# Four attention layers of 32 query heads: attention begins with a quarter of the keys, output products go in passes, and TensorE's order comes from other assumed durations

## The chip, the cores and the metric

The kernel runs on one core of a Trainium2 chip. The metric is the device time of one execution in microseconds (us). The kernel before takes 4103.47 us, the median of three runs (4100.76 to 4105.26). One further execution was profiled; its own time is 4101.9 us.

## The reference

The input x has 2048 rows of 512 numbers. Four layers follow one another; they use the weights A, B, A, B. A layer is x + attention(layernorm(x)) @ wo, with 32 query heads of 16 numbers each, and one head of keys and one of values that all query heads share:

```python
q = (x @ wq).reshape(B, S, H, Dh).transpose(0, 2, 1, 3)    # 32 heads of 16
k = x @ wk                                                  # one head of 16
v = x @ wv
p = softmax(einsum("bhqd,bkd->bhqk", q, k) * Dh ** -0.5)
o = einsum("bhqk,bkd->bhqd", p, v)                          # 2048 x 2048 per head
```

Per layer there are 32 x 2048 x 2048 exponentials, 134 million, and they are computed without a running maximum; a check at the end chooses a general path for inputs whose scores are too large, and that path does not run here.

## The kernel before, in words

A layer's queries are cut into four blocks of 512 rows (b = 0 to 3) and the 32 heads into four groups of eight (m = 0 to 3); a block and a group make a *pair*, and there are 64 pairs. The 2048 keys are cut into sixteen *key chunks* of 128. In a pair, even and odd heads are taken in turn (`odd`), four heads each; a pair and a parity with a range of key chunks is a *segment* (`segs`). For one key chunk of one segment there are:

- two *score steps* (S, in `scores`, line 500): each multiplies 128 keys with the queries of two heads, two matmuls side by side, into a tile `st` of 128 x 1024 in PSUM, of which there are three (NST);
- two exponentials on ScalarE (line 505), one for each `st`, 4096 in the whole kernel, into a tile `pt`, of which there are seven (NPT);
- one *value step* (P, in `pv`, line 520): eight matmuls that read the two `pt` and add four heads' products, with the sum of the exponentials beside them, to one bank `acc` of PSUM.

When a segment ends, `merge` adds `acc` to `num` and `den` on VectorE; after the pair's last segment it takes the reciprocal and writes `ot`.

Everything else is *background*: generators whose steps are put between S and P. A step of type M is three matmuls (`mm3`, lines 213 to 215), since float32 operands are split in two parts. `outputs` multiplies `ot` with wo (one M for each group and 128 rows), adds to the tile `xt` (line 364) and writes x to DRAM; `normed` does the layer norm of a block and four transposing steps (T, line 257); `keys_values` makes a block's keys and values in four M, one norm step (N, line 207) and one transposing step (V, line 304), with a chain on VectorE between; `queries` makes four M and an N for each group, writes them to DRAM, and `load_q` (line 383, eight DMAs on SyncE's queue) brings them back in the layout that S reads. `load_x` loads a block's x into four of six `xt` tiles, also on SyncE's queue.

The order of TensorE's instructions is written out when the program is built, by a loop that keeps a clock of its own: it adds an assumed duration for each step (`T_MM`, `T_S`, `T_P`), assumes when exponentials end (`T_EXP`), and chooses S, P or a background step. A background step may go ahead when `credit` is positive (each P earns RATE), while the first block of a layer still lacks its values (`urgent`), or when both S and P would have to wait (`stall`). `Background` has two queues, `first` and `later`; `need(key)` runs steps, `first` ahead of `later`, until the key is there, whatever the credit. Engines run their instructions in program order, so an instruction that waits holds up those behind it.

Before the loop, a preamble computes the normed rows of blocks 0 to 2, their keys and values, and the queries of pair 0. In each layer, the pair (b = 0, m = 0) is cut at key chunk 12, so that the last block's keys may come later.

Of the kernel before, what the change touches and what calls it, by code (L numbers as in the profile page):

```python
# [20 lines left out]
P = 128  # L21
S = 2048
# [12 lines left out]
NPT = 7  # L35
# [11 lines left out]
T_MM, T_S, T_P, T_EXP, SYNC, LATE = 225, 216, 1090, 973, 180, 270  # L47
RATE = 300


class Clock:


    def __init__(self):
        self.pe = 0
        self.dve = 0

    def mm(self, ns):
        self.pe += ns
# [5 lines left out]
class Background:  # L65
# [3 lines left out]
    def __init__(self, clk):  # L69
# [6 lines left out]
        self.ready = 0  # L76

# [3 lines left out]
    def add_later(self, *gens):  # L81
        self.later.extend(gens)

# [3 lines left out]
    def step(self):  # L87
        while self.left():
            if not self.open:
                self.queue = self.first or self.later  # L90
            try:
                self.clk.pe = max(self.clk.pe, self.ready)
                self.open, self.ready = next(self.queue[0])
# [18 lines left out]
def fast_path(ctx, tc, x_in, weights, out, flag):  # L112
# [7 lines left out]
    pts = ctx.enter_context(tc.tile_pool(name="pts", bufs=NPT))  # L120
# [77 lines left out]
    def copy(dst, src):  # L198
        if state["pool"] is None:
            V.tensor_copy(dst, src)  # L200
        else:
            nc.scalar.copy(dst, src)  # L202
# [8 lines left out]
    def mm3(ps, a, b, first, last):  # L211
# [4 lines left out]
        clk.mm(3 * T_MM)  # L216
# [3 lines left out]
    ot = {}  # L220

# [46 lines left out]
    def keys_values(l, b):  # L268

        i = l % 2  # L270
        xT = xnT[l, b]

# [5 lines left out]
        kf = one.tile([P, BQ], F32, name="kf")  # L278
# [36 lines left out]
    def queries(l, b, ms=range(NM), last=True):  # L315
# [5 lines left out]
        yield False, clk.dve + SYNC  # L321
        for m in ms:
# [25 lines left out]
            yield False, at  # L348

    def outputs(l, b, ms):  # L350

        w = wt["wo", l]
        yield False, clk.dve + SYNC
        last = NM - 1 in ms
        for t in range(4 * b, 4 * b + 4):
# [17 lines left out]
            if last and t == 4 * b + 3:  # L373
                bg.done.add(("x", l, b))
            yield False, clk.dve + SYNC
# [50 lines left out]
    slots = [(s, c, j) for s, (_, _, c0, c1) in enumerate(segs) for c in range(c0, c1)  # L426
             for j in (0, 2, 1, 3)]
    qt = {}
# [4 lines left out]
    def merge(s):  # L433
# [6 lines left out]
        if pr not in sums:  # L440
            sums[pr] = [one.tile([P, BQ], F32, name=n) for n in ("num", "den")]
# [10 lines left out]
        r = one.tile([P, BQ], F32, name="rec")  # L452
        if (l, b) > (0, 0):
            bg.need(("x",) + ((l, b - 1) if b else (l - 1, NB - 1)))
# [12 lines left out]
        if m == NM - 2:  # L467
            load_x(l, b)
        if b < NB - 1:
            if m == NM - 1:  # L470
                bg.add(outputs(l, b, range(NM)))
                if l < NL - 1:
                    bg.add(normed(l + 1, b), keys_values(l + 1, b))
                    bg.add_later(queries(l + 1, b))
        elif m == NM - 2:
            bg.add(outputs(l, b, range(NM - 1)))
        elif m == NM - 1:
# [280 lines left out]
```

## Time and profile before

| What | Value |
|---|---|
| median of 3 runs | 4103.47 us |
| the profiled execution's own time | 4101.9 us |
| its span on the core | 4100.1 us |
| TensorE (PE) matmul busy | 3916.7 us, 96% |
| ScalarE (ACT) busy | 3815.2 us, 93% |
| VectorE (DVE) busy | 1115.5 us, 27% |
| GpSimd (POOL) busy | 90.9 us, 2% |
| first exponential starts, last one starts | 60.5 us, 4079.4 us |

Busy time counts the stretch in which at least one instruction of the engine is under way. Matmuls overlap, and the end of one is modelled, so a TensorE that is 96% busy need not be working at its peak; distances from start to start say more. An exponential, too, may start while the one before it is still under way: its mean duration is 1314 ns, but 4096 of them make 3805.3 us of busy time.

### The profile page before, as it was taken

What the parts mean: (1) busy time and instruction counts of PE and PEld (TensorE: products, weight loads), DVE (VectorE), ACT (ScalarE), POOL (GpSimd) and SP (SyncE); (2) the same over time, 40 slices, a digit from 0 to 9 for tenths busy, and PEclk for the clock granted to TensorE, in tenths of its full rate; (3) what the DMA queues carried; (4) which work ended last, traced back from release to release, by engine and by line L of the source; (5) the groups of instructions that cost most, each with busy time, mean ns of one, the idle gap of its engine ahead of it and who ended that gap; (6) DMA issues with size and microseconds to landing.
All of it is one profiled execution on the core that took longest, in us unless ns stands there. A gap on an engine that the chain in (4) does not pass through costs nothing.

```text
span 4100.1 us, 65070 instructions
## 1 busy us (share of the span) xinstructions
PE 3916.7 (96%) x26707; PEld 1043.3 (25%) x26707; DVE 1115.5 (27%) x1770; ACT 3815.2 (93%) x4112; POOL 90.9 (2%) x101
## 2 busy tenths in 40 slices
PE   6999999999999999999999999999999999999998
PEld 3232222222221222222222222222222222121212
DVE  6333313232331321313233122131324211011112
ACT  4999999999999999999999999999999999999997
POOL 1000000000000000000000000000000000000000
PEclk8999999999999999999999999999999999999999
DMA  2010100000001000000001000000000100000000
GB/s 79 19 39 27 37 16 16 27 21 27 27 19 34 21 32 14 14 27 22 32 22 47 6 22 32 21 16 19 22 29 24 34 11 32 6 21 22 16 21 12
DMA packets 85877, 100.92 MB, mean 25 GB/s; under 512 B 14144, under 2 KB 63296, under 8 KB 85568
## 3 DMA queue, kind: packets, MB, share of 16 engines
q1 hardware_dynamic: 85248, 95.60, 7.1%
q8 instruction: 212, 3.47, 0.3%
q0 software_dynamic: 320, 1.05, 0.1%
q14 instruction: 97, 0.79, 0.1%
HBM read 63.05 MB, written 33.55 MB: 24 GB/s over the span
## 4 chain that ended last, share of the span: by engine, by line
PE 54%; ACT 35%; issue 8%; DVE 3%; DMA 0%; ACTq 0%; POOL 0%; SPq 0%; DVEq 0%; POOLq 0%
ACT pt L505 35%; PE acc L520 23%; PE st L500 17%; PE qps L213 2%; PE ops L213 2%; PE qps L214 1%; PE qps L215 1%; PE ops L214 1%; PE ops L215 1%; PE tps L257 1%; PE gps L207 1%; PE kps L213 0%; PE kps L214 0%; PE kps L215 0%; DVE ko L291 0%
## 5 line engine op out<-in xcount | busy, mean ns | idle before, releaser
L505 ACT ACTIVATE pt<-st 128x1024 f32<-128x1024 f32 x4096 | 3805.3, 1314 | 219.9 <-PE st L500 205.6
L520 PE MATMUL acc<-pt,vop 128*32 128x512 f32 x16384 | 2167.6, 604 | 4.5 <-DVE gv L309 4.5
L500 PE MATMUL st<-qt,kop 64*128 64x512 f16 x8192 | 1491.5, 383 | 131.7 <-ACT pt L505 3.3
L500 PEld LDWEIGHTS <-kop 64*128 64x128 f16 x8192 | 368.4, 93 | 2201.8 <-issue 2183.2
L520 PEld LDWEIGHTS acc<-pt,vop 128*32 128x32 f32 x16384 | 331.5, 108 | 587.8 <-issue 579.2
L446 DVE SCALAR_TENSOR_TENSOR num<-acc,half,num 128x512 f32<-128x512 f32 x72 | 54.1, 751 | 1048.5 <-PE acc L520 1048.5
L461 DVE RECIPROCAL den<-den 128x512 f32<-128x512 f32 (+1 forms) x76 | 216.3, 2847 | 2.2
L364 DVE TENSOR_TENSOR xt<-ops,xt 128x512 f32<-128x512 f32 x76 | 52.5, 691 | 565.4 <-PE ops L215 565.4
L443 DVE TENSOR_SCALAR num<-acc,half 128x512 f32<-128x512 f32 x64 | 48.0, 751 | 540.7 <-PE acc L520 540.7
L330 DVE TENSOR_SCALAR q<-qps 128x512 f32<-128x512 f32 x64 | 44.2, 691 | 492.5 <-PE qps L215 492.5
L213 PE MATMUL qps<-xnT,wq 128*128 128x512 f32 x256 | 119.1, 465 | 0.8 <-ACT xnT L202 0.7
L213 PE MATMUL ops<-wo,ot 128*128 128x512 f32 x252 | 116.7, 463 | 2.0 <-DVE xt L364 2.0
L214 PE MATMUL qps<-xnT,wq 128*128 128x512 f32 x256 | 101.9, 398 | 0.2 <-DVE xnT L262 0.2
L215 PE MATMUL qps<-xnT,wq 128*128 128x512 f32 x256 | 101.4, 396 | 0.0
L214 PE MATMUL ops<-wo,ot 128*128 128x512 f32 x252 | 99.4, 394 | 0.0
L215 PE MATMUL ops<-wo,ot 128*128 128x512 f32 x252 | 98.7, 392 | 0.0
L332 POOL TENSOR_TENSOR sq<-q 128x512 bf16<-128x512 f32 x64 | 66.5, 1039 | 1442.4 <-DVE q L330 1442.4
L337 DVE SCALAR_TENSOR_TENSOR q<-gps,q 128x512 f32<-128x512 f32 x64 | 44.1, 689 | 110.1 <-PE gps L207 110.1
L257 PE MATMUL tps<-ident,xn 128*128 128x128 f32 x256 | 44.3, 304 | 26.6 <-DVE xn L247 26.6
L213 PEld LDWEIGHTS qps<-xnT,wq 128*128 128x128 f32 x256 | 48.3, 189 | 65.1 <-issue 46.1
L213 PEld LDWEIGHTS ops<-wo,ot 128*128 128x128 f32 x252 | 47.0, 187 | 57.0 <-issue 46.0
L200 DVE CAST xnT<-tps 128x512 fp32r<-128x512 f32 x52 | 35.9, 690 | 71.1 <-PE tps L257 71.1
(91 smaller groups left out, 1108.8 us busy)
## 6 DMA issues: line engine op xcount, KB each, us to landing
qt<-qs SPq DMA_DIRECT2D x512, 64.0 KB, 2.3
qs<-qs SPq DMA_DIRECT2D x64, 256.0 KB, 2.1
xs<-xt SPq DMA_DIRECT2D x48, 256.0 KB, 2.0
xt<-xs SPq DMA_DIRECT2D x48, 256.0 KB, 3.9
xt<-in_A_x_dram SPq DMA_DIRECT2D x32, 256.0 KB, 3.6
out_dram<-xt SPq DMA_DIRECT2D x16, 256.0 KB, 2.1
wst<-in_A_wo_dram SPq DMA_DIRECT2D x8, 256.0 KB, 2.7
wst<-in_B_wq_dram SPq DMA_DIRECT2D x8, 256.0 KB, 3.0
```

The source lines that it names most:

```text
L213: PE.matmul(ps, a[0], b[0], start=first, stop=False)
L214: PE.matmul(ps, a[0], b[1], start=False, stop=False)
L215: PE.matmul(ps, a[1], b[0], start=False, stop=last)
L257: PE.transpose(ps[:, c * P:(c + 1) * P], xn[:, c * P:(c + 1) * P], ident)
L332: G.tensor_tensor(sq, q, q, ALU.mult)
L364: V.tensor_tensor(x, ps, x, ALU.add)
L443: V.tensor_scalar(t, a, k, None, ALU.mult)
L446: V.scalar_tensor_tensor(t, a, k, t, ALU.mult, ALU.add)
L461: V.reciprocal(den[:, c], den[:, c])
L500: PE.matmul(st[:, k * 512:(k + 1) * 512], kop[l % 2][c // 4][r, (c % 4) * P:(c % 4 + 1) * P], qt[pr][r, 2 * (j % 2) + odd], start=True, st ...
L505: nc.scalar.activation(pt[:, :n], st[:, :n], AF.Exp, scale=SCALE / UP / UP)
L520: PE.matmul(acc[s][32 * j:32 * j + 32, :], vop[l % 2][c // 4][:, c % 4, 16 * odd:16 * odd + 32], pt[:, k * 512:(k + 1) * 512], start=(c == ...
```

## The change

- The planner's durations: S (`T_MM`) 216 ns, an M's matmul (`T_MR`) 231, P 860 (was 1090), the distance of exponentials 904 (was 973), and a table CHANGE of what a change between S, P and M adds. A step is chosen only if, by the planner's clock, TensorE is back at S before ScalarE runs out (`fits`, with 100 ns of slip). The old rules (`stall`, `fed`, `last_p`) go.
- `segs`: in layer 0 the three pairs of block 0 with m = 0 to 2 take turns over four quarters of the keys; in layers 1 to 3 the pairs m = 0 and 1 of block 0 take turns, key chunks 0 to 11 and then 12 to 15. `num` and `den` have three buffers for it, and a pair's queries are loaded again for each turn.
- The preamble makes only block 0's normed rows, keys and values, and pair 0's queries; blocks 1 to 3 go to the background.
- `outputs` goes in passes: groups 0 and 1 after m = 1, groups 2 and 3 after m = 3 (in block 3, group 2 and group 3 by themselves). `load_x` goes from the merge of m = 2 to that of m = 1. `hurry` moves the next block's `queries` from `later` to the end of `first`, ahead of the `normed` that is added then.
- `pt` is one tile with eight slots, and the dependency of an exponential on the one eight before it is dropped.

```diff
-NPT = 7
+NPT = 8
-T_MM, T_S, T_P, T_EXP, SYNC, LATE = 225, 216, 1090, 973, 180, 270
-RATE = 300
+T_MM, T_MR, T_P, T_EXP, T_END, LEAD, SYNC, LATE = 216, 231, 860, 904, 1020, 487, 60, 270
+CHANGE = {"SP": 93, "PS": 114, "SM": 200, "PM": 200, "MS": 105, "MP": 105}
+RATE, SLIP = 300, 100
...
+    def mm(self, ns, mode="M"):
+        self.pe += self.change(mode) + ns
+        self.mode = mode
+
+    def act(self):
+        self.exp.append(max(self.exp[-1] + T_EXP if self.exp else 0, self.pe - T_MM + LEAD))
...
+    def hurry(self, gen):
+
+        if gen in self.later:
+            self.later.remove(gen)
+            self.first.append(gen)
...
-    for pr, (l, b, m) in enumerate(pairs):
-        cuts = [0, NK]
-        if b == 0 and m == 0:
-            cuts = [0, 12, NK]
-        for c0, c1 in zip(cuts, cuts[1:]):
-            for odd in range(2):
-                segs.append((pr, odd, c0, c1))
+    for l in range(NL):
+        first = 16 * l
+        n, cuts = (3, [0, 4, 8, 12, NK]) if l == 0 else (2, [0, 12, NK])
+        segs += [(p, odd, c0, c1) for c0, c1 in zip(cuts, cuts[1:]) for p in range(first, first + n)
+                 for odd in range(2)]
+        segs += [(p, odd, 0, NK) for p in range(first + n, first + 16) for odd in range(2)]
...
-        if m == NM - 2:
+        last = b == NB - 1
+        if m == 1:
             load_x(l, b)
...
+            bg.add(outputs(l, b, [0, 1]))
+        elif m == 2 and last:
+            bg.add(outputs(l, b, [2]))
+        elif m == 3:
+            bg.add(outputs(l, b, [3] if last else [2, 3]))
             if l < NL - 1:
+
+                bg.hurry(qs_of[l + (b + 1) // NB, (b + 1) % NB])
+                bg.add(normed(l + 1, b), keys_values(l + 1, b))
...
-            if j == 0 and c == (0 if pr else 12) and odd and pr + 1 < len(pairs):
-                qt.pop(pr - 1, None)
-                qt[pr + 1] = load_q(*pairs[pr + 1])
+            if j == 0 and s in loads and c == c1 - 3:
+                qt[segs[s + 1][0]] = load_q(*pairs[segs[s + 1][0]])
...
+        if len(exps) >= NPT:
+            tc.declare_no_dep(e, exps[-NPT], reason="behind the reads in between")
...
-        for b in range(NB - 1):
-            run(kv[b], NC)
-            if b == 0:
-                run(q0)
-            if b < NB - 2:
-                run(normed(0, b + 1))
-            run(kv[b])
+        run(kv[0], 1 + NC)
+        run(q0)
+        run(kv[0])
...
-        bg.add(queries(0, 0, range(1, NM)), normed(0, 3), kv[3],
-               load_split(("wo", 0), weights[0][3]))
+        bg.add(queries(0, 0, [1, 2], False))
+        for b in range(1, NB):
+            if b == NB - 1:
+                bg.add(queries(0, 0, [3]))
+            bg.add(normed(0, b), kv[b])
+        bg.add(load_split(("wo", 0), weights[0][3]))
...
+            urgent = b == 0 and ("v", l, NB - 1) not in bg.done
+            now = clk.pe
+
+            free = sum(e + T_END + SYNC <= now for e in clk.exp[nxt - NST:]) if nxt >= NST else NST
+            s_at = max(now, clk.exp[nxt - NST] + T_END + SYNC) if nxt >= NST else now
+            dry = clk.exp[-1] + T_EXP - LEAD if clk.exp else now
...
+            def fits(mode, ns):
+                return now + clk.change(mode) + ns + CHANGE[mode + "S"] <= max(dry, s_at) + SLIP
+
+            near = c > c1 - 1 - (bg.size + 2) // 2
+            m_ok = bg.can() and (not near or bg.open) and (
+                urgent or credit > 0 or min(s_at, p_at) > now + 300 or near and bg.open)
+            if forced:
+                what = "P"
+            elif free and (clk.mode == "S" or free > 1):
+                what = "S"
+            elif m_ok and fits("M", 3 * T_MR):
+                what = "M"
+            elif p_at <= now and fits("P", T_P):
+                what = "P"
+            elif free:
+                what = "S"
```

More of the change, by code (lines that the diff above doesn't have):

```diff
@@ L92, in step @@
                 self.clk.pe = max(self.clk.pe, self.ready)
-                self.open, self.ready = next(self.queue[0])
+                self.open, self.ready, *size = next(self.queue[0])
+                if not self.open:
+                    self.size = size[0] if size else 1
                 return True
@@ L220, in fast_path @@
     ot = {}
+    qs_of = {}
     def load_x(l, b):
@@ L277, in keys_values @@
                 yield True, clk.pe
-        kf = one.tile([P, BQ], F32, name="kf")
+        kf = one.tile([P, BQ], F32, name="tmp")
         V.stream_shuffle(kf, ps, upper)
@@ L372, in outputs @@
                     xt[l + 1, t] = x
-            if last and t == 4 * b + 3:
-                bg.done.add(("x", l, b))
-            yield False, clk.dve + SYNC
+            if t == 4 * b + 3:
+                bg.done.update(("o", l, b, m) for m in ms)
+            yield False, clk.dve + SYNC, len(ms)
     def load_q(l, b, m):
@@ L440, in merge @@
         if pr not in sums:
-            sums[pr] = [one.tile([P, BQ], F32, name=n) for n in ("num", "den")]
+            sums[pr] = [one.tile([P, BQ], F32, name=f"{n}{pr % 3}") for n in ("num", "den")]
             for t, k in zip(sums[pr], f):
@@ L570, in fast_path @@
             l, b, m = pairs[pr]
-            urgent = b == 0 and m == 0 and ("v", l, NB - 1) not in bg.done
-            s_at = max(clk.pe, exp_end[nxt - NST] + SYNC if nxt >= NST else 0)
-            p_at = max(clk.pe, exp_end[chunk_of[ready[0]]] + SYNC) if ready else 1e12
-            forced = ready and chunk_of[ready[0]] <= nxt - NPT
-            stall = min(s_at, p_at) > clk.pe + 100
-            fed = exp_end[-1] - clk.pe if exp_end else 0
-            due = credit > 0 and (not last_p or credit > 2000) or urgent or stall
@@ L578, in fast_path @@
-            if bg.can() and (c < c1 - 3 and due or bg.open and (c >= c1 - 3 or due)):
-                before = clk.pe
-                bg.step()
-                credit -= clk.pe - before
-                last_p = False
-            elif (nxt == len(chunks) or forced or (s_at > clk.pe + 60 and p_at < s_at)
-                  or last_p and p_at <= clk.pe and fed >= T_P + W // 2 * T_S + LATE):
-                last_p = True
+            urgent = b == 0 and ("v", l, NB - 1) not in bg.done
+            now = clk.pe
@@ new lines, in fast_path @@
+            free = sum(e + T_END + SYNC <= now for e in clk.exp[nxt - NST:]) if nxt >= NST else NST
+            s_at = max(now, clk.exp[nxt - NST] + T_END + SYNC) if nxt >= NST else now
+            dry = clk.exp[-1] + T_EXP - LEAD if clk.exp else now
+            if nxt == len(chunks):
+                free, s_at, dry = 0, 1e12, 1e12
+            p_at = max(now, clk.exp[chunk_of[ready[0]]] + T_END + SYNC) if ready else 1e12
+            forced = ready and chunk_of[ready[0]] <= nxt - NPT + 1
+            def fits(mode, ns):
+                return now + clk.change(mode) + ns + CHANGE[mode + "S"] <= max(dry, s_at) + SLIP
@@ new lines, in fast_path @@
+            near = c > c1 - 1 - (bg.size + 2) // 2
[11 more added lines that the diff above has]
+                what = "S"
+            elif p_at < s_at:
+                what = "P" if fits("P", p_at - now + T_P) or s_at > 1e11 else "S"
+            else:
+                what = "S"
@@ L586, in fast_path @@
+            if what == "M":
+                bg.step()
+                credit -= clk.pe - now
+            elif what == "P":
                 clk.pe = p_at
```

67 lines of the change are left out of this document (32 added, 35 removed).

## The prediction

> **What bounds the kernel now.** I first read the whole span, then ScalarE, because the 4096 exponentials are the longest work that can't be shortened here.
>
> ```profile
> PE 3916.7 (96%) x26707; PEld 1043.3 (25%) x26707; DVE 1115.5 (27%) x1770; ACT 3815.2 (93%) x4112; POOL 90.9 (2%) x101
> L505 ACT ACTIVATE pt<-st x4096: 1017/1150/1807, 60.5 to 4079.4; 128x1024 f32<-128x1024 f32 x196
> ```
> ```profile
> 2507.45 100.94 ACT L505 ACTIVATE pt<-st 128x1024 f32<-128x1024 f32 x110 [2.60 <-PE st L500]
> 3233.18 123.85 ACT L505 ACTIVATE pt<-st 128x1024 f32<-128x1024 f32 x135 [1.90 <-PE st L500]
> ```
>
> The first exponential takes 1.02 us and ends at 61.5. In the two unbroken rows each further one adds (123.85 - 1.02) / 134 = 0.9166 us, in the other row the same. So the floor of ScalarE is 4095 x 0.9167 = 3753.9 us. The last exponential ends at about 4080.6, so from first end to last end it takes 4019.1 us: **265 us are lost there**, 61.5 us pass before, 19.5 after it, and 1.8 us lie outside the span (4101.9 against 4100.1). The planner's new 904 ns is a little less than this 917.
>
> Where the 265 us are lost, I read from windows cut at the layers (the second fence counts only M steps, by their first matmul):
>
> ```profile
> 61.00:1091.00 1030.00, 999.01 (x6803) 281.33 (x6801) 301.40 (x459) 953.78 (x1025) 32.09 (x31) 1.00 0.08 26
> 1091.00:2098.00 1007.00, 976.32 (x6686) 257.00 (x6685) 280.20 (x434) 953.58 (x1026) 20.65 (x20) 1.00 0.07 24
> 2098.00:3104.00 1006.00, 975.34 (x6680) 256.79 (x6676) 280.17 (x434) 952.56 (x1026) 20.65 (x20) 1.00 0.07 24
> 3104.00:4080.00 976.00, 928.63 (x6419) 224.49 (x6412) 192.47 (x275) 944.18 (x1024) 5.16 (x5) 1.00 0.06 20
> 2230.00:2340.00 110.00, 102.94 (x723) 21.69 (x721) 23.18 (x31) 110.00 (x122) 0.00 (x0) 1.00 0.11 32
> ```
> ```profile
> 61.00:1091.00 1030.00, 83.28 (x184) 34.60 (x183) 1.00 0.08 26
> 1091.00:2098.00 1007.00, 67.20 (x144) 26.85 (x144) 1.00 0.07 24
> 3104.00:4080.00 976.00, 38.79 (x84) 15.67 (x84) 1.00 0.06 20
> ```
>
> A layer has 1024 exponentials, 938.7 us at the floor. The layers take 1030, 1007, 1006 and 976: losses of 91, 68, 67 and 37. In the window at 2230, which has no background, ScalarE is busy for all of 110.00 us: nothing is lost. The loss comes with the background. The ScalarE row at 2507 shows how: 2.60 us of idle time, ended by a score. What TensorE did before it:
>
> ```profile
> 2500.61 0.39 PE L207 MATMUL gps<-sq,bones 128*128 128x512 bf16 x1
> 2500.94 0.39 PE L500 MATMUL st<-qt,kop 64*128 64x512 f16 x2
> 2501.26 1.06 PE L520 MATMUL acc<-pt,vop 128*32 128x512 f32 x8
> 2502.25 0.61 PE L500 MATMUL st<-qt,kop 64*128 64x512 f16 x4
> 2502.79 0.50 PE L213 MATMUL qps<-xnT,wq 128*128 128x512 f32 x1
> ...
> 2503.70 1.06 PE L520 MATMUL acc<-pt,vop 128*32 128x512 f32 x8
> 2504.69 0.50 PE L213 MATMUL qps<-xnT,wq 128*128 128x512 f32 x1
> ...
> 2506.96 0.82 PE L500 MATMUL st<-qt,kop 64*128 64x512 f16 x6
> ```
> ```profile
> 2405.20 0.65 PE L257 MATMUL tps<-ident,xn 128*128 128x128 f32 x4
> 2405.78 0.39 PE L500 MATMUL st<-qt,kop 64*128 64x512 f16 x2
> ```
>
> P and three M in a row, from 2503.70 to 2506.96, with no score between. From starts to starts: a P costs 0.99 us, two S with the change to what follows 0.54, an M between S and P 0.91, three M in a row 2.27 (0.76 each), N 0.33, T 0.58. S to a change takes 0.32 (2500.94 to 2501.26), so S to S is 0.54 - 0.32 = 0.22.
>
> **TensorE's need.** Per P there are two S and two exponentials: 0.99 + 0.54 = 1.53 us, against 1.833 on ScalarE. So TensorE has 0.30 us left per P, 155 us for a layer's 512. A lone M between two S adds 0.32 + 0.91 - 0.22 = 1.01, between S and P 0.91; I take 0.99, since the new order mostly puts it behind a first S, and 0.76 as its other end. The background of layers 1 and 2 is 144 M x 0.99 = 142.6 us; 20 N and 4 V (bounded by N) at 0.32 + 0.33 - 0.22 = 0.43, and 16 T at 0.68, make 21. Sum 164 against 155: TensorE is short by 9 us per layer if each M stands alone, and by nothing if a third stand in rows. Layer 3 has 84 M, 83 us: no shortage. Layer 0 has 184, and 8 more come from the preamble (blocks 1 and 2's keys): 190, with some 40 N and V and 24 T 223, short by 68. But 48 M that are the next layer's queries can move on, from layer to layer, into layer 3's slack. What stays short is 68 + 9 + 9 - 48 = **about 38 us**, where 265 are lost now. That is the room for another order.
>
> **The change, part by part.**
>
> *Earlier start.* The path to the first score:
>
> ```profile
> 18.23 0.50 PE L213 MATMUL qps<-xnT,wq 128*128 128x512 f32 x1 [0.68 <-ACT xnT L202]
> 23.58 0.66 DVE L189 SCALAR_TENSOR_TENSOR wq<-wst,wq 128x512 fp32r<-128x512 f32 x1
> 24.84 0.69 DVE L330 TENSOR_SCALAR q<-qps 128x512 f32<-128x512 f32 x1
> 26.07 0.86 DVE L247 TENSOR_SCALAR xn<-xt,mv,rstd 128x512 f32<-128x512 f32 x1
> 27.18 0.68 DVE L337 SCALAR_TENSOR_TENSOR q<-gps,q 128x512 f32<-128x512 f32 x1
> 31.02 0.68 DVE L262 TENSOR_TENSOR xnT<-tps,xnT 128x512 fp32r<-128x512 f32 x1
> 32.33 0.38 SPq L346 DMA_DIRECT2D qs<-qs  x1
> 34.46 3.61 SPq L383 DMA_DIRECT2D qt<-qs  x8
> 37.30 0.68 DVE L296 SCALAR_TENSOR_TENSOR kop<-gps,ko 128x512 f16<-128x512 f32 x1
> 59.70 0.68 PE L500 MATMUL st<-qt,kop 64*128 64x512 f16 x2 [2.32 <-DVE gv L309]
> ```
> ```profile
> qt<-qs SPq DMA_DIRECT2D x512, 64.0 KB, 2.3
> ```
>
> Pair 0's queries are in place at 34.46 + 3.61 + 2.3 = 40.4, block 0's keys at 38.0; the 19 us until 59.70 are blocks 1 and 2. Between 24.84 and 32.33 VectorE also works for them, 0.86 + 0.68 in the rows at 26.07 and 31.02. Without that I put the first score at 38.7, and the first exponential's end, 1.8 later as now, at 40.5: **21 us less**. Bounds: 18 (VectorE saves nothing) to 24.
>
> What is moved costs elsewhere. Its M, N, T are in the need above. Its chain is now in the loop, as block 3's is today:
>
> ```profile
> 87.75 1.40 SPq L225 DMA_DIRECT2D xt<-in_A_x_dram  x3
> 97.20 0.65 PE L257 MATMUL tps<-ident,xn 128*128 128x128 f32 x4 [2.65 <-DVE xn L247]
> 115.97 0.69 DVE L296 SCALAR_TENSOR_TENSOR kop<-gps,ko 128x512 f16<-128x512 f32 x1
> ```
>
> From the loads of x at 87.75 to the keys at 116.7 it takes 29 us. The first quarter gives ScalarE 48 exponentials, 44 us, and before this chain the queue holds two groups of queries, some 8 us each by the rows 24.84 to 32.33: 45 us. And a group of four M may begin only at the first P of a segment of four key chunks (`near`), which adds waits. So the second quarter begins late; I take 8 us. Pair 1's queries have 16 exponentials, 14.7 us, and need 4 M (2.8), 7.5 on VectorE and GpSimd, 2.1 to write, 5.9 to load: 18, late by 3. The load of x, for which TensorE's T waited 2.65 us in the row at 97.20, comes three times instead of once; it stands ahead of pair loads on SyncE's queue: 7. With about 3 of slow clock (below) the start costs **21 us** (10 to 40).
>
> *The planner's order.* It puts an M only where S can follow before ScalarE runs dry. Its prices: S S P 1499 (the rows: 1530), exponentials 904 (917), M alone 998 (990). The first two are low by 1 to 2%, so they nearly cancel. RATE lets it place 300 ns of background per P, just what TensorE has left. But one block of layers 1 and 2 needs, at its own prices, 36 x 998 + 5 N x 737 + 4 T x 951 + V, 44 us, and gets 128 x 300 = 38. The 6 us left over, queries for the most part since they stand in `later`, are forced at the block's end by `load_q`'s `need`, in a row: 6 M, then N behind GpSimd's and VectorE's 2 us. All S and P stand behind that N on TensorE, and ScalarE holds at most three scores. I take 3 us at each of 12 block ends: **36** (0, if `min(s_at, p_at) > now + 300` gives enough free places, to 100). The rows bunched there are cheap: about 80 M at 0.76 instead of 0.99 return some 20 of the 38, which leaves **18** of shortage (0 to 38).
>
> *Layer ends.* The last block's chain (merge, outputs, norm, keys) has 48 P, 88 us, before key chunk 12 is wanted; it had 24, 44 us. Its length was 29 us from a load of x, and here some 10 us of merge and outputs stand ahead: hidden by S and P of two pairs. Uncovered, it would cost up to 40. I keep **5** for three ends.
>
> *At nothing.*
>
> ```profile
> L364 DVE TENSOR_TENSOR xt<-ops,xt 128x512 f32<-128x512 f32 x76 | 52.5, 691 | 565.4 <-PE ops L215 565.4
> L446 DVE SCALAR_TENSOR_TENSOR num<-acc,half,num 128x512 f32<-128x512 f32 x72 | 54.1, 751 | 1048.5 <-PE acc L520 1048.5
> ```
>
> The passes of `outputs` add 64 additions on line 364 and the shorter segments 22 merges of two operations each, 44 + 33 us of VectorE, hidden by its 73% idle time; the M are as many as before. Fifteen more loads of queries (3.61 us of SyncE each) stand beside an idle queue. Seven to eight `pt`, and the dropped dependency: ScalarE waited for itself 4.3 us in all, so 0 to 5, taken as 0:
>
> ```profile
> ACT pt L505 <- ACT pt L505: 4.3, 19, 0.3
> ```
>
> One tile with eight slots could make every exponential wait for every P; but in this trace the first query M starts before the last piece of wq is written, so slices are followed one by one.
>
> *The tail* (19.5) is the same work.
>
> **Sum.** 40.5 + 3753.9 + (21 + 36 + 18 + 5 = 80) + 19.5 + 1.8 = **3896 us**. The profiled execution is 1.6 us below the median of the runs; I correct nothing for it.
>
> **A rule against a row.** After the idle time ahead of 59.70 the clock was low:
>
> ```profile
> 60.00:70.00 10.00, 9.31 (x43) 4.81 (x41) 1.93 (x4) 5.08 (x6) 1.04 (x1) 0.74 0.00 0
> ```
>
> At 0.74 of ten us, with the rest full, 2.6 us of work were lost, my 3 above. The Trainium skill ("TensorE: Matmul & The Clock Gate", Part 1) says that the clock halves after an idle window and returns after about 3.4 us of work: 1.7 us lost, and the sum would be 3895. The Trainium skill ("ScalarE: Activation LUTs", What ACT_TABLE_LOAD costs) gives 186 ns + 0.833 ns per element, less 93 for overlap: an estimate of 946 ns for 1024 elements. By that the floor alone would be 3874 and the time 4016, but the rows say 917 and the measurement decides, so this gets no chance below.
>
> **Rivals.**
> 1. *ScalarE never starves*: the planner's chained M cover the shortage, and block ends fit. Only the start's 21 remain: 3837. For it speaks the window at 2230; against it the 44 against 38 us per block.
> 2. *The order still loses about as much as now*: need-driven bunches and VectorE's latency leave 170 to 240: 3985 to 4055. For it: bunches like 2504.69 also come from urgent and waiting rules, which stay. Against: the new rule looks at ScalarE each time.
> 3. *SyncE's queue turns it slower*: `load_x` now goes out at m = 1 and wants two `xt` tiles that `normed` of the block before holds, and `hurry` puts 16 M of queries ahead of that `normed`. Behind the waiting load, on one queue, stand the writes and loads of the next pair's queries, for which TensorE, then ScalarE wait. If it stops 14 us at each of 15 blocks, (4103 - 3896) / 15, the kernel is not faster; at a whole norm, 20 us, it gives 4196. For it: the queue is in order, and 24 M at one per 3.4 P end near P 80 of 128, while the load goes out at P 64. Against: group 3's queries are wanted only at P 96, 30 us later.
> 4. *The start does not move*: the preamble's path isn't shortened. Then 19 more: 3915.
>
> **How the numbers follow.** Chances: forecast (3855 to 3965) 0.62, rival 1 0.10, rival 2 0.16, rival 3 0.08, rival 4 0.04. Under rival 2 a few hundredths end at no change. This kernel can tell about 0.2%, 8 us, from no change. Faster: 0.89; within: 0.02; slower: 0.09. The low end, 3835, is rival 1 with its start; the high end adds the upper bounds of the start (19 more) and block ends (64 more) half of the layer ends' (20) and half of the shortage's (10): 4009, so 4010.
>
> **What will show it.** First exponential near 39.5; unbroken ScalarE rows still at 0.917 apiece; loss per layer about 43, 17, 15 and 5 instead of 91, 68, 67 and 37; M spread one by one between scores; idle time of ScalarE at block ends, behind N or query loads. If the first exponential is not before 45, or layer 3 loses more than 15, or SyncE's load of x stands for tens of us ahead of query loads, I am wrong at that step.

## The result and the profile after

The changed kernel takes 3962.74 us, the median of its runs (3961.86 to 3963.3); the kernel before took 4104.36 us beside it. The ratio is 0.9656, with a 95% interval of 0.9644 to 0.9668: **3.4% faster, 141 us**. The forecast was 3896 us with a range of 3835 to 4010, so the sign and the range held and the point was 67 us too low. The profiled execution took 3962.37 us.

The page of the changed kernel, first the share of each engine, then groups of instructions, then one row of the DMA issues:

```profile
PE 3843.3 (97%) x26707; PEld 974.0 (25%) x26707; DVE 1196.9 (30%) x1890; ACT 3797.6 (96%) x4102; POOL 88.6 (2%) x99
...
L525 PE MATMUL st<-qt,kop 64*128 64x512 f16 x8192 | 1393.2, 384 | 61.5 <-DMA qt<-qs 23.4
...
L389 DVE TENSOR_TENSOR xt<-ops,xt 128x512 f32<-128x512 f32 x140 | 96.8, 691 | 742.1 <-PE ops L238 742.1
...
qt<-qs SPq DMA_DIRECT2D x632, 64.0 KB, 2.3
```

VectorE got 81 us more to do; the additions on line 389, 140 instead of 76, are 44 of them. The 632 loads of queries instead of 512 are fifteen more of eight DMAs each, as forecast, and all scores together waited 23.4 us for such loads in the whole kernel, 9.8 of them before the first exponential. The exponential, now on line 530:

```profile
L530 ACT ACTIVATE pt<-st x4096: 1016/1072/1865, 39.9 to 3939.4; 128x1024 f32<-128x1024 f32 x196
L530 ACTq EVENT_SEMAPHORE  x1: 7119/7119/7119, 32.7 to 32.7; - x1
```

The first one starts at 39.9 (60.5 before) and ends at 40.9. The last one ends at 3940.9, and 19.6 follow it. From first end to last end it takes 3900.0 us, of which 4095 x 0.9167 = 3753.9 is the floor: **146 us are lost, where 265 were before and 80 were forecast**. Head, floor and tail are as forecast to half a us, so the whole error lies in this term.

The windows of the changed kernel, cut at the first 180 us of exponentials and then at the layers (us, then busy us and instructions of PE, PEld, DVE, ACT, POOL, the granted clock, DMA share, GB/s), and the same windows for the M steps alone, by their first matmul:

```profile
40.00:220.00 180.00, 153.60 (x978) 43.80 (x976) 78.24 (x142) 135.11 (x144) 6.17 (x6) 0.92 0.18 55
220.00:1053.00 833.00, 822.72 (x5753) 209.19 (x5753) 259.03 (x384) 816.10 (x882) 17.57 (x17) 1.00 0.08 26
1053.00:2025.00 972.00, 958.80 (x6702) 243.08 (x6702) 299.49 (x464) 948.75 (x1024) 22.74 (x22) 0.99 0.08 26
2988.00:3940.00 952.00, 927.08 (x6494) 221.34 (x6490) 220.58 (x320) 943.47 (x1023) 10.36 (x10) 1.00 0.07 23
```
```profile
40.00:220.00 180.00, 11.67 (x24) 5.15 (x24) 0.92 0.18 55
220.00:1053.00 833.00, 62.01 (x129) 24.03 (x129) 1.00 0.08 26
1053.00:2025.00 972.00, 73.17 (x152) 28.31 (x152) 0.99 0.08 26
2025.00:2988.00 963.00, 75.14 (x156) 29.07 (x156) 1.00 0.09 27
2988.00:3940.00 952.00, 49.45 (x103) 19.19 (x103) 1.00 0.07 23
```

In the first 180 us ScalarE is busy for 135 us only, at a TensorE clock of 0.92; behind them it is busy for 98 to 99%. Layers 1 to 3 fell from 1007, 1006 and 976 us to 972, 963 and 952.

For all kernels below I worked out the same loss: from the end of one exponential to the end of a later one, less 0.9167 us for each between them. In us, from the profiled executions:

| Kernel | first exponential starts | loss, first 192 | rest of layer 0 | layer 1 | layer 2 | layer 3 | sum |
|---|---|---|---|---|---|---|---|
| before | 60.5 | 29 | 63 | 68 | 68 | 39 | 265 |
| forecast | 39.5 | 21 | 22 | 17 | 15 | 5 | 80 |
| after | 39.9 | 55 | 19 | 34 | 24 | 15 | 146 |
| e1: start undone | 64.0 | 46 | 21 | 23 | 24 | 8 | 121 |
| e2: two blocks first | 49.7 | 10 | 21 | 35 | 24 | 16 | 106 |
| e3: order undone | 39.8 | 56 | 79 | 62 | 62 | 33 | 293 |
| e4: passes undone | 39.4 | 55 | 37 | 36 | 31 | 18 | 177 |
| e5: prices | 39.4 | 52 | 34 | 18 | 25 | 16 | 144 |
| e6: no slip | 39.3 | 55 | 16 | 38 | 27 | 28 | 163 |
| e8: dependency kept | 39.3 | 56 | 19 | 36 | 24 | 16 | 150 |
| e9: groups begin earlier | 39.5 | 55 | 36 | 38 | 34 | 33 | 197 |
| e10: more queries first | 48.0 | 18 | 21 | 34 | 24 | 16 | 112 |
| e11: M not behind S | 49.5 | 34 | 73 | 61 | 60 | 48 | 277 |
| e12: e2 with e5's prices | 49.9 | 10 | 24 | 18 | 25 | 16 | 93 |
| e13: order alone | 59.7 | 44 | 35 | 31 | 32 | 18 | 160 |

The first 192 exponentials are those of three pairs, the ones that take turns in the kernel after. The forecast's layer 0 is its start term and the remainder. A profiled execution lies up to 7 us from its kernel's median.

**The first 192.** The rows of ScalarE in the changed kernel, with the idle time in front of each in brackets:

```profile
59.45 1.94 ACT L530 ACTIVATE pt<-st 128x1024 f32<-128x1024 f32 x2 [3.50 <-PE st L525]
...
81.44 1.02 ACT L530 ACTIVATE pt<-st 128x1024 f32<-128x1024 f32 x1 [4.50 <-PE st L525]
...
114.40 2.86 ACT L530 ACTIVATE pt<-st 128x1024 f32<-128x1024 f32 x3 [14.50 <-PE st L525]
...
121.89 39.52 ACT L530 ACTIVATE pt<-st 128x1024 f32<-128x1024 f32 x43 [1.15 <-PE st L525]
165.15 1.94 ACT L530 ACTIVATE pt<-st 128x1024 f32<-128x1024 f32 x2 [3.73 <-PE st L525]
...
224.15 2.86 ACT L530 ACTIVATE pt<-st 128x1024 f32<-128x1024 f32 x3 [8.05 <-PE st L525]
```

Five long stops: for pair 1's queries (3.50), for pair 2's (4.50), and for the keys of the second, third and fourth quarter (14.50, 3.73, 8.05); together 34 of the 55, with small ones between. The row of 43 shows the floor again: (39.52 - 1.02) / 42 = 0.9167. What stood before the second quarter's keys:

```profile
53.74 0.50 PE L236 MATMUL qps<-xnT,wq 128*128 128x512 f32 x1
...
57.34 0.37 PE L525 MATMUL st<-qt,kop 64*128 64x512 f16 x1 [1.94 <-DMA qt<-qs]
59.02 0.60 PE L525 MATMUL st<-qt,kop 64*128 64x512 f16 x3 [1.31 <-DMA qt<-qs]
...
63.99 0.50 PE L236 MATMUL qps<-xnT,wq 128*128 128x512 f32 x1
...
75.40 3.58 SPq L408 DMA_DIRECT2D qt<-qs  x8
79.02 1.85 SPq L249 DMA_DIRECT2D xt<-in_A_x_dram  x4
...
91.04 0.66 PE L281 MATMUL tps<-ident,xn 128*128 128x128 f32 x4
...
104.65 0.63 PE L238 MATMUL kps<-xnT,wkv 128*128 128x512 f32 x1
105.08 0.63 PE L236 MATMUL kps<-xnT,wkv 128*128 128x512 f32 x1
...
107.91 0.39 PE L237 MATMUL kps<-xnT,wkv 128*128 128x512 f32 x1
108.14 0.40 PE L238 MATMUL kps<-xnT,wkv 128*128 128x512 f32 x1
```

Group 2's queries begin at 53.74 and go on at 63.99 only, after a gap of 10 us, in which TensorE's scores wait 1.94 and 1.31 us for pair 1's queries. SyncE's queue then writes and loads those queries, and the first load of block 1's x goes out behind them, at 79.02, 39 us after the first exponential. Its transposes follow at 91.04, its M at 103.96 to 108.5, and the stop ends at 114.40.

**Behind the first 192** the loss is 91 us. A row of M steps at the end of a segment, and the wait at a layer's key chunk 12, in the same kernel:

```profile
1306.93 1.07 PE L550 MATMUL acc<-pt,vop 128*32 128x512 f32 x8
1307.93 0.50 PE L236 MATMUL qps<-xnT,wq 128*128 128x512 f32 x1
...
1308.75 0.40 PE L236 MATMUL qps<-xnT,wq 128*128 128x512 f32 x1
...
1309.54 0.61 PE L525 MATMUL st<-qt,kop 64*128 64x512 f16 x4
1309.97 2.87 ACT L530 ACTIVATE pt<-st 128x1024 f32<-128x1024 f32 x3 [1.52 <-PE st L525]
```
```profile
1148.43 1.11 PE L525 MATMUL st<-qt,kop 64*128 64x512 f16 x4 [1.97 <-DVE kop L321]
1149.15 1.94 ACT L530 ACTIVATE pt<-st 128x1024 f32<-128x1024 f32 x2 [5.68 <-PE st L525]
```

A group of M steps collects in a bank of PSUM that the next segment needs for `acc`, so `pv` closes an open group (`bg.close`) at a segment's border: two M follow the P of 1306.93, and the score comes 2.61 us after that P. I counted all places where an exponential ends late, by what TensorE did before its score: 19 places with two or three M behind a P, 27 us together; the wait at 1149.15, 5.8 us; 291 places of about 0.15 us, where a score behind one P comes a little late, 44 us (the expectation of e5 below puts 48 us to them); 12 single M behind a P, 7 us; and 7 us of the rest.

The 291 small delays are 68, 86, 81 and 56 in the rest of layer 0 and in layers 1 to 3, with 10, 14, 12 and 8 us. The windows above count 129 M from 220 to 1053 and 152, 156 and 103 in the layers, so there are 0.52 to 0.57 of these delays for each M, in every layer. In 201 of the 291, a single M between two scores stands just ahead of that P.

### The profile page after: what moved, and what is told of

Read it like the earlier page. It is cut to its first block, busy times and chain, and to the rows that moved or that the text cites. A ratio compares the mean times of both kernels' runs of the same rounds, so it can differ in the third digit from the quotient of the medians.

```text
span 3960.5 us, 61194 instructions
## 1 busy us (share of the span) xinstructions
PE 3843.3 (97%) x26707; PEld 974.0 (25%) x26707; DVE 1196.9 (30%) x1890; ACT 3797.6 (96%) x4102; POOL 88.6 (2%) x99
## 4 chain that ended last, share of the span: by engine, by line
PE 70%; ACT 26%; DVE 2%; DMA 1%; SPq 0%; issue 0%; POOL 0%; DVEq 0%; POOLq 0%
PE acc L550 37%; ACT pt L530 26%; PE st L525 21%; PE ops L236 2%; PE qps L236 2%; PE qps L238 1%; PE qps L237 1%; PE ops L238 1%; PE ops L237 1%; PE tps L281 1%; PE gps L230 1%; SPq L408 0%; PE kps L236 0%; DVE q L355 0%; DMA qt<-qs 0%
## 5 line engine op out<-in xcount | busy, mean ns | idle before, releaser
L550 PE MATMUL acc<-pt,vop 128*32 128x512 f32 x16384 | 2191.3, 607 | 11.3 <-DVE q L355 5.9
L525 PE MATMUL st<-qt,kop 64*128 64x512 f16 x8192 | 1393.2, 384 | 61.5 <-DMA qt<-qs 23.4
L525 PEld LDWEIGHTS <-kop 64*128 64x128 f16 x8192 | 317.3, 93 | 2042.9 <-issue 2007.9
L389 DVE TENSOR_TENSOR xt<-ops,xt 128x512 f32<-128x512 f32 x140 | 96.8, 691 | 742.1 <-PE ops L238 742.1
L472 DVE SCALAR_TENSOR_TENSOR num<-acc,half,num 128x512 f32<-128x512 f32 x94 | 70.3, 748 | 410.4 <-PE acc L550 410.4
L472 DVE SCALAR_TENSOR_TENSOR den<-acc,half,den 128x512 f32<-128x512 f32 x94 | 69.7, 742 | 0.0
```

The lines of the kernel that those rows point to most:

```text
L389: V.tensor_tensor(x, ps, x, ALU.add)
L472: V.scalar_tensor_tensor(t, a, k, t, ALU.mult, ALU.add)
L525: PE.matmul(st[:, k * 512:(k + 1) * 512], kop[l % 2][c // 4][r, (c % 4) * P:(c % 4 + 1) * P], qt[pr][r, 2 * (j % 2) + odd], start=True, st ...
L550: PE.matmul(acc[s][32 * j:32 * j + 32, :], vop[l % 2][c // 4][:, c % 4, 16 * odd:16 * odd + 32], pt[:, k * 512:(k + 1) * 512], start=(c == ...
```

## The experiments

Two theories stood at first. By the one the forecast failed at the start: blocks 1 to 3 come too slowly in the loop, and the earlier first exponential is given back. By the other it failed in the order: TensorE still has too little time behind each P, or its planner reckons with wrong durations. Times are medians; a ratio is that to the kernel before in the same call, with its 95% interval. For the kernel after it is 0.9656 (0.9644 to 0.9668).

**e1: the start undone.** Three blocks are made before the loop again, and layer 0 has the cuts of before.

```diff
-        n, cuts = (3, [0, 4, 8, 12, NK]) if l == 0 else (2, [0, 12, NK])
+        n, cuts = (1, [0, 12, NK]) if l == 0 else (2, [0, 12, NK])
...
-        run(kv[0], 1 + NC)
-        run(q0)
-        run(kv[0])
+        for b in range(3):
+            run(kv[b], 1 + NC)
+            if b == 0:
+                run(q0)
+            if b < 2:
+                run(normed(0, b + 1))
+            run(kv[b])
```

> The changed kernel with its start undone: the preamble makes blocks 0 to 2 as before, and layer 0 cuts only its first pair, at key chunk 12; the order, the output passes and the rest stay. Theory A (the early start gains 20.6 us at the first exponential, but its first 192 exponentials lose 55 us where the kernel before lost 29, since the chains of queries and keys do not fit into quarters): first exponential at 60 us, the first 192 lose 25 to 32, time 3950 to 3960, so not slower than the changed kernel's 3963. Theory B (the early start is a plain gain; what is lost in its quarters is background work that has to be done anyway and returns elsewhere): 3975 to 3985.

Measured: 3960.94 us, 0.9651 (0.9635 to 0.9667), no different from the kernel after. The first exponential starts 24.1 us later and 25 us fewer are lost behind it: 6 of them in layer 0, and 19 in layers 1 and 3, for which no run shows the reason. So against this start, "attention begins with a quarter of the keys" brought nothing. But e1 doesn't run the start as the kernel before ran it. Its first 192 exponentials lose 46 us, where 29 were lost before and 25 to 32 were expected, and most of them in one stop at key chunk 12, which waits for block 3's keys:

```profile
115.51 1.91 SPq L249 DMA_DIRECT2D xt<-in_A_x_dram  x4
...
148.74 1.94 ACT L530 ACTIVATE pt<-st 128x1024 f32<-128x1024 f32 x2 [38.86 <-PE st L525]
```

Three groups of queries stand ahead of that block's norm, and its x is loaded at 115.51 only. Under the new order both starts lose to a late chain, so e1 doesn't show what an early start is worth when its chain is in time.

**e2: half of it.** Blocks 0 and 1 before the loop, and layer 0's turns cut at key chunks 8 and 12.

```diff
-        n, cuts = (3, [0, 4, 8, 12, NK]) if l == 0 else (2, [0, 12, NK])
+        n, cuts = (3, [0, 8, 12, NK]) if l == 0 else (2, [0, 12, NK])
...
+        for b in range(2):
+            run(kv[b], 1 + NC)
+            if b == 0:
+                run(q0)
+            if b < 1:
+                run(normed(0, b + 1))
+            run(kv[b])
```

> As the changed kernel, but the preamble makes blocks 0 and 1, and three pairs of layer 0 take turns over key chunks 0 to 7, 8 to 11, 12 to 15. Theory A (the loss comes from chains that are longer than a turn of 44 us; a first turn of 88 us covers them): first exponential near 51 us, the first 192 lose 20 to 30, time 3935 to 3950, the best of the three starts. Theory B (plain gain of an early start): between the other two starts, 3968 to 3975.

Measured: 3925.93 us, 0.9565 (0.9549 to 0.9581), 37 us less than the kernel after. The first exponential is 9.8 us later, and the first 192 lose 10 us instead of 55. The window of e2 from its first exponentials on, of a length with that of after:

```profile
50.00:228.00 178.00, 171.91 (x1200) 43.82 (x1197) 78.02 (x132) 169.39 (x184) 5.13 (x5) 0.98 0.19 56
```

ScalarE is busy for 169 of 178 us, where it was for 135 of 180, and TensorE's clock is at 0.98 instead of 0.92. A first turn of eight key chunks gives three pairs 96 exponentials, 88 us, and that covers the two groups of queries and the chain of block 2; the 44 us of a quarter didn't cover those groups and the chain of block 1. e2 changes two things, the length of the turn and block 1's chain, which now runs before the loop, and it doesn't part them.

**e3: the order undone.** The constants and the loop of before in the frame of the changed kernel.

```diff
-T_MM, T_MR, T_P, T_EXP, T_END, LEAD, SYNC, LATE = 216, 231, 860, 904, 1020, 487, 60, 270
+T_MM, T_S, T_P, T_EXP, SYNC, LATE = 225, 216, 1090, 973, 180, 270
```

> The changed kernel with the order undone: the planner's prices and rules of before (973 for an exponential, 1090 for a P, no price for a change of work, no look at when ScalarE runs dry); start, turns, output passes and eight slots stay. Theory A (the order is what lowers the loss of layers 1 to 3 from 68, 68, 39 to 34, 24, 15): those losses return to 60, 60, 35, time 4060 to 4090. Theory B (the passes and the turns spread the background, and the order has little to do): 3970 to 4000.

Measured: 4108.78 us, 1.001 (1.0 to 1.002). With the old order, everything else together is worth nothing. Who ended ScalarE's idle time (us, times, the longest), in e3 and then in the kernel after:

```profile
ACT pt L523 <- PE st L518: 252.5, 326, 17.3
```
```profile
ACT pt L530 <- PE st L525: 119.9, 109, 14.7
```

Three times as many stops; beyond layer 0's start every stretch of the table loses about twice what it does after, or more.

**e4: the passes undone.** `outputs` and `load_x` at the places of before (in block 3 the groups 0 to 2 at m = 2, group 3 at m = 3).

```diff
-        if m == 1:
+        if m == 2:
             load_x(l, b)
-            bg.add(outputs(l, b, [0, 1]))
-        elif m == 2 and last:
-            bg.add(outputs(l, b, [2]))
+            if last:
+                bg.add(outputs(l, b, [0, 1, 2]))
         elif m == 3:
-            bg.add(outputs(l, b, [3] if last else [2, 3]))
+            bg.add(outputs(l, b, [3] if last else range(NM)))
```

> The changed kernel with the output passes undone: all four groups' products after m = 3 (in block 3 groups 0 to 2 after m = 2, group 3 after m = 3), the load of x at m = 2 again; start and order stay. Theory A (TensorE's work bounds layers 0 to 2, and its amount is the same): within 8 us of 3963. Theory B (the passes level the background over a block, and without them it queues up and is forced in rows at block ends): 15 to 50 us slower, 3978 to 4013, with the loss in rows of M at block ends.

Measured: 3994.05 us, 0.9731 (0.9715 to 0.9747): the passes are worth 31 us. A place of e4's timeline:

```profile
887.75 1.07 PE L549 MATMUL acc<-pt,vop 128*32 128x512 f32 x8
888.74 0.50 PE L236 MATMUL ops<-wo,ot 128*128 128x512 f32 x1
...
891.70 0.82 PE L524 MATMUL st<-qt,kop 64*128 64x512 f16 x6
...
892.13 5.61 ACT L529 ACTIVATE pt<-st 128x1024 f32<-128x1024 f32 x6 [2.34 <-PE st L524]
```

Here a group for 128 rows has four M, one for each group of heads, and all four stand in a row behind the P, 2.96 us from 888.74 to the score. With passes a group has two, or one in block 3.

**e5: the measured prices.** P at 884 and exponentials at 917, as the ends in the trace have them.

```diff
-T_MM, T_MR, T_P, T_EXP, T_END, LEAD, SYNC, LATE = 216, 231, 860, 904, 1020, 487, 60, 270
+T_MM, T_MR, T_P, T_EXP, T_END, LEAD, SYNC, LATE = 216, 231, 884, 917, 1020, 487, 60, 270
```

> The changed kernel, with two of the planner's prices set to what the traces show: P 884 ns (with the change to S 998) instead of 860, the distance of exponentials 917 instead of 904. After the first 220 us the changed kernel loses 101 us on ScalarE, 48 of them in 291 places of about 0.17 us where one P stands between scores. Theory A (both errors nearly cancel, and TensorE's work bounds the layers 0 to 2): within 8 us of 3963. Theory B (the small losses come from the prices): they fall by half or more, time 3930 to 3945.

Measured: 3957.51 us, 0.9646 (0.9629 to 0.9662), no different. Layer 1 loses 15 us less and the rest of layer 0 loses 15 us more. The small late scores are as many as before, 280 instead of 291 and 47 us instead of 44, so the wrong prices did not make them.

**e6: no slip.**

```diff
-RATE, SLIP = 300, 100
+RATE, SLIP = 300, 0
```

> The changed kernel with SLIP = 0 instead of 100 ns: a step is placed only if the planner's clock sees no dry ScalarE at all. Theory A (TensorE's work is the bound; what is not placed in time is forced in rows at the ends of segments): within 8 us of 3963, with fewer places of 0.1 to 0.2 us and more rows of M at segment ends. Theory B (the slip is paid in full at each of the 291 places): 25 to 40 us faster, 3923 to 3938.

Measured: 3978.76 us, 0.9699 (0.9683 to 0.9715): slower by 16 us than the kernel after. The small late scores stay, 296 with 43 us, and in layers 1 to 3 the stops at key chunk 12 grow to 19, 6 and 6 us. Less freedom for the M does not remove the small delays; it makes the last block's keys late.

**e8: the dependency kept.**

```diff
-        if len(exps) >= NPT:
-            tc.declare_no_dep(e, exps[-NPT], reason="behind the reads in between")
```

> The changed kernel without the dropped dependency: an exponential again waits for the one eight before it, which has long ended. Theory A (the wait costs nothing, as I predicted): 3958 to 3967, and unbroken rows of exponentials at 917 ns each. Theory B (one more wait on ScalarE's queue lengthens each exponential): 5 to 50 us slower, with a longer distance in unbroken rows.

Measured: 3964.72 us, 0.9663 (0.9647 to 0.9679): no difference. ScalarE's queue in e8:

```profile
L530 ACT ACTIVATE pt<-st x4096: 1013/1067/1805, 39.3 to 3943.2; 128x1024 f32<-128x1024 f32 x196
L530 ACTq EVENT_SEMAPHORE  x4089: 17/17/7085, 32.2 to 3942.8; - x195
```

Each exponential from the ninth on has a wait of 17 ns more in front of it, 4089 in all where there was one, and exponentials still end 917 ns apart.

**e9: groups of four M begin earlier,** so that none is open at a segment's border.

```diff
-            near = c > c1 - 1 - (bg.size + 2) // 2
+            near = c > c1 - 1 - (bg.size + 2) // 2 - (3 if bg.size > 1 and c1 - c0 > 8 else 0)
```

> The changed kernel, but in segments of sixteen or twelve key chunks a group of four M may not begin in the last six P instead of the last three. In the changed kernel 19 places with two or three M in a row right after a segment's last P lose 27 us after the first 220 us. Theory A (these rows are groups that were begun too late, and are forced to close when the segment's bank is handed over): they vanish, 10 to 27 us faster, 3935 to 3953. Theory B (what isn't begun there is forced by the next need instead): within 8 us of 3963, or slower.

Measured: 4012.3 us, 0.9781 (0.9764 to 0.9797): 50 us slower than after. The rows behind a segment's last P did go, from 19 places with 27 us to four with 5, so nearly all of them come from groups that are closed there. But the background falls behind, and the last block's keys are late at each layer:

```profile
1171.93 0.77 PE L236 MATMUL kps<-xnT,wkv 128*128 128x512 f32 x1 [1.60 <-DVE xnT L286]
...
1175.88 0.39 PE L236 MATMUL kps<-xnT,wkv 128*128 128x512 f32 x1
...
1181.14 0.69 DVE L321 SCALAR_TENSOR_TENSOR kop<-gps,ko 128x512 f16<-128x512 f32 x1
...
1182.60 2.85 ACT L530 ACTIVATE pt<-st 128x1024 f32<-128x1024 f32 x3 [19.14 <-PE st L525]
```

The scores of key chunk 12 are next in TensorE's order, and behind them stands everything; ScalarE stops for 19.14 us here, and for 19.2 and 19.3 in the next two layers.

**e10: two more groups of queries before the loop,** so that block 1's norm and keys come first in the background.

```diff
-        q0 = queries(0, 0, [0], False)
+        q0 = queries(0, 0, [0, 1, 2], False)
...
-        bg.add(queries(0, 0, [1, 2], False))
```

> The changed kernel, but the preamble also makes the queries of groups 1 and 2 of block 0, so that the background begins with block 1's norm and keys. In the changed kernel ScalarE stops 3.6 us at pair 1, 4.6 at pair 2, 14.6 at the second quarter, 3.8 at the third and 8.2 at the fourth. Theory A (the queries ahead of block 1's chain in the queue are what makes it late, with its x loaded only at 79 us): the first two stops go, the third falls below 5; the first exponential comes 5 to 8 us later; the first 192 lose 25 to 33 instead of 55, time 3940 to 3950. Theory B (the chain by itself is longer than a quarter): the third stop stays at 10 or more, the first 192 lose 40 or more, time 3955 to 3970.

Measured: 3937.98 us, 0.96 (0.9584 to 0.9616): 25 us less than after, with the quarters kept. ScalarE's rows in e10, with the keys of block 1 among them:

```profile
48.02 4.69 ACT L530 ACTIVATE pt<-st 128x1024 f32<-128x1024 f32 x5 [21.23 <-PE st L525]
...
86.40 9.52 ACT L530 ACTIVATE pt<-st 128x1024 f32<-128x1024 f32 x10 [0.42 <-PE st L525]
...
89.79 0.69 DVE L321 SCALAR_TENSOR_TENSOR kop<-gps,ko 128x512 f16<-128x512 f32 x1 [1.69 <-PE gps L230]
```

The first exponential is 8 us later, but block 1's keys stand at 90.5 instead of 113.6, and the stop of 14.50 us is gone. With nothing ahead of them in SyncE's queue, the loads of block 1's x go out from 3.8 to 15.3 us, where they stood at 79.02. So e10 takes the two groups out of the way of the chain on TensorE and on SyncE at once.

**e11: no M directly behind a score,** with a slip of 250, on the kernel of e12 below. From starts to starts in the kernel after, an M between two scores adds 0.99 us and one between a P and a score 0.90, and I tried to save the difference.

```diff
-RATE, SLIP = 300, 100
+RATE, SLIP = 300, 250
...
-            elif m_ok and fits("M", 3 * T_MR):
+            elif m_ok and (clk.mode != "S" or min(s_at, p_at) > now + 300) and fits("M", 3 * T_MR):
```

> The start with blocks 0 and 1 in the preamble, the planner's prices P 884 and exponential 917, SLIP 250, and a background step may not follow a score directly unless both S and P have to wait; so M stands behind a P, between P and S, where it adds 0.895 us to TensorE's work instead of 0.987 between two S. Theory A (TensorE's work bounds layers 0 to 2, some 450 M there gain 0.09 us each, and ScalarE starves no more than that bound): 15 to 40 us faster than the same kernel with free places, that is 3885 to 3910. Theory B (2.2 us from score to score, by P and M, is more than three score tiles cover, and each M starves ScalarE by 0.1 to 0.2 us on top): 3930 to 3990.

Measured: 4097.93 us, 0.9986 (0.9976 to 0.9995). The idea failed. Behind the first 192, the exponential behind a P and an M ends late 370 times by about 0.06 us and 39 times, mostly behind two or three M in a row, by about 1.7 (24 and 68 us). The layers' ends stop for 16.5 us each, and the scores wait 63 us for loads of queries instead of 23, so the background also comes too late. That three `st` give too little lead for an M behind a P is an argument and not shown, since the slip was changed along with the rule.

**e12: e2 and e5 together.** The edits are theirs.

```diff
-T_MM, T_MR, T_P, T_EXP, T_END, LEAD, SYNC, LATE = 216, 231, 860, 904, 1020, 487, 60, 270
+T_MM, T_MR, T_P, T_EXP, T_END, LEAD, SYNC, LATE = 216, 231, 884, 917, 1020, 487, 60, 270
...
+        n, cuts = (3, [0, 8, 12, NK]) if l == 0 else (2, [0, 12, NK])
...
+        for b in range(2):
```

> The start with blocks 0 and 1 in the preamble and the planner's prices P 884 and exponential 917, SLIP 100: the base of the run with M behind P. Theory A (the prices cancel, TensorE is the bound): 3918 to 3930, as with the prices of the changed kernel (3926). Theory B (with the start out of the way the prices count): under 3915.

Measured: **3915.19 us, 0.9541 (0.9525 to 0.9557)**, 47 us under the kernel after and the best of all. Its interval overlaps that of e2, so what the prices add is not settled; by the table they take 17 us from layer 1, as they did in e5, and give 3 back in layer 0.

**e13: the order alone.** The start of e1, the passes of e4 and the dependency of e8, with the new planner and eight `pt`.

```diff
+        n, cuts = (1, [0, 12, NK]) if l == 0 else (2, [0, 12, NK])
...
+            bg.add(outputs(l, b, [3] if last else range(NM)))
...
-            tc.declare_no_dep(e, exps[-NPT], reason="behind the reads in between")
```

> The order by itself: the start of before (three blocks in the preamble, only the first pair of layer 0 cut, at key chunk 12), the output passes of before and the kept dependency, with the changed kernel's planner, prices and eight slots. Theory A (the parts add up: passes 31 us, start 0, dependency 2 beside an order that brings the rest): 3961 + 31 + 2, so 3985 to 4000. Theory B (the order needs the passes or the start to bring anything): above 4040. Theory C (without the short turns the passes bring little): 3960 to 3975.

Measured: 4002.84 us, 0.9755 (0.9739 to 0.9771). The order by itself is worth 101 us, although its first 192 have the stop of e1 again, 36.95 us here. The turns of layers 1 to 3, `hurry` and the eighth `pt` count with it, because no run undoes them. The passes are worth some 31 on top of it (e4), the start and the dependency nothing that can be told (e1, e8). These make about 132 of the 141; the 9 left are little more than the intervals. Parts need not add up: without the new order (e3) the rest was worth nothing.

## Why the prediction was right or wrong

- **Head, floor and tail** were right: 40.9, 3753.9 and 19.6 us against 40.5, 3753.9 and 19.5. With them fell rival 4, that the start doesn't move, and rival 1, which had no loss but the start's. Rival 2 asked for 170 to 240 us of loss; 146 lies between it and the forecast.
- **"The start costs 21 us"** was mis-sized: 55. The mechanism was named rightly, a queue with two groups of queries ahead of the chain. The term that failed is the 16 us for those two groups, which with the chain's 29 made 45 against the quarter's 44. Block 1's x goes out 39 us after the first exponential, since SyncE's queue sends it only behind the groups' writes and loads, at 79.02, and in between TensorE stood still for pair 1's queries. From there to the keys it takes 34.6 us instead of 29. So the second quarter begins 74.5 us after the first exponential, which is 30 of the 55. I named a price for one late quarter, and three were late: the third began 7 us later than its 44 us of exponentials allow, and the fourth 15. e10 takes the queries out of the chain's way, e2 gives it a longer turn; each removes 37 to 45 us of the 55. `near` is not seen as a cause: it keeps a group from beginning, and group 2 had begun. The slow clock is part of this loss, but no run parts it from the late chain. The 7 us for the load of x had no ground in the row at 97.20, whose T waited for VectorE's `xn`.
- **"Block ends 36 us"**, forced by `load_q`'s `need`: the size was near, 27, but by luck, because the cause was another. The rows at the ends are groups closed at a segment's border, as e9 shows. The planner's prices in this bullet were also too high: by its constants a norm step is 216 + 200 + 105 = 521 ns and a T 430 + 305 = 735, which leaves a block with 42 us against 38.
- **"Shortage 18 us"** was mis-sized: about 58 are left when the rows and the layer's end are taken off. I let 48 M go on into layer 3 and had 20 us returned by rows. The windows count 152, 156 and 103 M in layers 1 to 3, where 144, 144 and 84 stood: 19 came into layer 3. With these amounts the prediction's own account, 0.99 an M and 21 for the small steps against 155 us, leaves layer 1 short by 16, layer 2 by 20, and the stretch from 220 to 1053 (129 M, 882 exponentials, so 441 x 0.30 = 132 us of room) by about 17: 53 us, near the 58. But the layers don't bear it out. By the same account layer 3 has 32 us of room (103 x 0.99 + 21 = 123 of 155), and yet it has 56 of the 291 small delays, as many for each M as the others. Its 15.3 us of loss are also the sign of being wrong that the prediction gave, more than 15. So what stands in place of the shortage is a loss of about 0.08 us (44 / 540) for each M, whether the sum leaves room or not. e5 and e6 leave it as it is, so neither the two prices nor the slip makes it. What does is open; no run takes the work away.
- **"Layer ends 5 us"** was right, 5.8, but by a thin margin: in e6, e9 and e11 they cost 6 to 19 us each.
- **"At nothing"** was right for the dependency and the fifteen loads, and wrong for the passes. I looked at what they add on VectorE, which is hidden as said, and not at what they do to the order: they make groups of M half as long, so less is forced in a row. e4 measures 31 us.
- **Rival 3**, SyncE's queue stopped by the load of x at every block, is not seen: the scores' waits for query loads are 23.4 us in all. At the first block the queue does matter, in the other direction: there x stands behind the queries. Rival 4's sum was off by 2: it adds 19 us where the start's step is 21.

What stays open: why each M loses its 0.08 us; how the 55 us split between the late chain and the slow clock; and whether M at cheap places would help if more than three `st` lay ahead, which was not tried.

## What to carry to other kernels

When work is moved from before a loop into it, draw up its chain with everything that stands ahead of it on each queue, and compare that with the work that is to cover it: a first turn twice as long with one block more before the loop (e2), or the chain put first (e10), was worth 25 to 37 us here, the early start with its late chain nothing. Splitting background into shorter groups can be worth more than its extra instructions cost, where an unfinished group is forced at a border. And a sum of work against room wants a stage with room as its test: here the small losses went with the number of background steps, in the layer with room too.

## What the hardware showed that was not expected

- After TensorE has waited, the chain that it waited for runs slower. In the changed kernel the keys' M at 104.65 and 105.08 stand 0.43 us apart and those at 107.91 and 108.14 0.23. The windows with them and ahead of them:

```profile
100.00:104.00 4.00, 0.67 (x5) 0.49 (x5) 2.93 (x5) 0.00 (x0) 0.00 (x0) 1.00 0.37 115
104.00:108.00 4.00, 4.00 (x11) 3.14 (x12) 0.00 (x0) 0.00 (x0) 0.00 (x0) 0.57 0.00 0
```

  TensorE is busy for 0.67 of 4 us, and in the next four the granted clock is 0.57; the matmuls at 0.43 last from 104.27 to 107.64, 3.4 us. In e9 the keys' M take 0.77 and 0.63 us from 1171.93 on, and 0.39 from 1175.88. In e1's long stop the granted clock is 0.50 from 118 to 140. The Trainium skill ("TensorE: Matmul & The Clock Gate", Part 1) says that the clock halves after an idle window and that it takes about 3.4 us of work to come back; by that rule, the trace agrees.
- Along an unbroken row exponentials start 904 ns apart and end 917 ns apart (medians of the changed kernel), so they last longer and longer, 1016 ns at the least and 1865 at the most. In the row of 135 of the kernel before they level off at about 1800 ns from the 60th on, with starts 918 apart in the mean. The planner's 904 is the distance of starts; the floor goes by the ends.
- 4088 more waits of 17 ns in ScalarE's queue (e8) cost no time that could be measured.
